# Group normalization that streams 268 MB: stores and loads taking turns in runs of three in place of two

## The chip, the cores and the metric

The kernel runs on one core of a Trainium2 chip, beside no other work. The metric is the device time of one execution in microseconds (us).

The instruction queues that matter are TensorE (PE, matmul), VectorE (DVE), ScalarE (ACT), GpSimd (POOL) and SyncE (SP). SP issues all large transfers. The transfers themselves are carried out by 16 DMA engines, each of which works through its own part of every transfer in the order of issue. A transfer has landed when the last of the 16 has finished its part.

## The reference, cut to what matters

```python
B, C, H, W = 128, 1024, 32, 16          # bfloat16
xr  = x.reshape(B, 32, 32, H, W)        # 32 groups of 32 channels
mu  = xr.mean(axis=(2, 3, 4), keepdims=True)
var = ((xr - mu) ** 2).mean(axis=(2, 3, 4), keepdims=True)
xn  = (xr - mu) / jnp.sqrt(var + 1e-5)
return xn.reshape(B, C, H, W) * g[None, :, None, None] + b[None, :, None, None]
```

The input is 134.2 MB and so is the output. One row of 16,384 values (one sample, one group) lies on one partition, so a tile of 128 partitions is four samples, 4.19 MB, and there are 32 tiles.

## The kernel before

Each tile is loaded, its mean is taken on PE and DVE, its squares about the mean on ACT, and it is scaled in place by DVE, POOL and ACT and stored. There are six tile buffers, so load `i + 6` has to wait until store `i` has landed. "Quarters" means that a tile is moved by four transfers of a quarter each; the squares of the first and of the last tile, which are loaded in quarters, are taken about the first quarter's mean, so that ACT can start early (`shifted`).

```python
XBUFS = 6
UPFRONT = 6
RUN = 2
...
def L(i):                                  # load tile i, issued by SP
    xt = xpool.tile([P, F], BF16, name="xt")
    parts = NQ if i == 0 or i >= NT - 1 else 1
    w = F // parts
    for c in range(parts):
        chain("sp", nc.sync.dma_start(out=xt[:, c*w:(c+1)*w], in_=x_v[i][:, c*w:(c+1)*w]))
    state[i] = {"xt": xt}

for i in range(min(UPFRONT, NT)):          # six loads before anything else
    L(i)
...
def shifted(i):
    return i == 0 or i == NT - 1
...
def M(i):                                  # 32 matmuls with an identity: sums on PE
    if shifted(i):
        matmuls(st, "pa", 0, MQ); matmuls(st, "pb", MQ, NMM)
    else:
        matmuls(st, "pa", 0, NMM)
...
def finish(i):
    if i < 0 or in_parts(i):               # the last two tiles are stored in quarters by A
        return
    for k in range(KC - LAST_SHARE, KC):
        scale_on("act", i, k)
    S(i, 0, NQ)                            # store tile i, issued by SP
    state.pop(i)
    if i % RUN == RUN - 1:
        first = i + 1 + UPFRONT - RUN
        for j in range(first, min(first + RUN, NT)):
            L(j)

M(0); R0(0); GB(); R1(0)
for i in range(NT):
    Q(i)                                   # squares on ACT; calls finish(i - 1) in its middle
    if i + 1 < NT:
        M(i + 1)
        R0(i + 1)                          # mean of the NEXT tile, on DVE
    V(i)                                   # 1/sqrt, scale and shift of tile i
    A(i)                                   # scaling of tile i
```

`chain` keeps the written order on each queue. SP's order is therefore: loads 0 to 5, stores 0 and 1, loads 6 and 7, stores 2 and 3, loads 8 and 9, and so on to loads 30 and 31, and then the last six stores.

Of the kernel before, what the change touches and what calls it, by code (L numbers as in the profile page):

```python
# [16 lines left out]

XBUFS = 6
UPFRONT = 6
RUN = 2  # L20
MM_FREE = 512
QUARTERS = 4
STORE_IN_PARTS = 2
# [6 lines left out]
def kernel(  # L30
# [21 lines left out]
    NT = B0 // NS  # L52
# [5 lines left out]
    NQ = QUARTERS  # L58
# [26 lines left out]
    def chain(key, inst):  # L85
        prev = last.get(key)
        if prev is not None:
            tc.add_manual_dep(inst.ins, prev.ins.name, nosync, reason="pipeline order")
        last[key] = inst
        return inst  # L90

    state = {}

    def L(i):
        xt = xpool.tile([P, F], BF16, name="xt")
        parts = NQ if i == 0 or i >= NT - 1 else 1
        w = F // parts
        for c in range(parts):
            chain(
                "sp",  # L100
                nc.sync.dma_start(  # L101
                    out=xt[:, c * w : (c + 1) * w], in_=x_v[i][:, c * w : (c + 1) * w]
                ),
            )
        state[i] = {"xt": xt}

    for i in range(min(UPFRONT, NT)):
        L(i)
# [35 lines left out]
    def GB():  # L144
# [9 lines left out]
            ),  # L154
        )
        chain("dve", nc.vector.tensor_copy(out=gb[:], in_=gb_p[:]))  # L156

    def shifted(i):
        return i == 0 or i == NT - 1

    def matmuls(st, name, lo, hi):
        ps = pspool.tile([P, MMN], F32, name=name)
# [13 lines left out]
    def M(i):  # L176
        st = state[i]
        if shifted(i):
            matmuls(st, "pa", 0, MQ)
            matmuls(st, "pb", MQ, NMM)  # L180
        else:
            matmuls(st, "pa", 0, NMM)
# [18 lines left out]
    def R0(i):  # L201
        st = state[i]
        if shifted(i):
            st["q"] = sum_of(st["pa"], None, "q")
        else:
            st["negmean"] = sum_of(st["pa"], None, "negmean")

    def R1(i):
        st = state[i]
        if not shifted(i):  # L210
            return
        st["negmean"] = sum_of(st["pb"], st["q"][:], "negmean")
        off = spool.tile([P, 1], F32, name="off")
        chain(
            "pool",
            nc.gpsimd.tensor_scalar(  # L216
                out=off[:],
                in0=st["negmean"][:],
                scalar1=1.0 / NQ,
                scalar2=st["q"][:],  # L220
                op0=ALU.mult,
                op1=ALU.subtract,
            ),
        )
        seed = spool.tile([P, 1], F32, name="seed")
        chain(
            "pool",
            nc.gpsimd.tensor_scalar(
                out=seed[:],
                in0=off[:],  # L230
                scalar1=-1.0,
                scalar2=off[:],
                op0=ALU.mult,
                op1=ALU.mult,
            ),
        )
        st["seed"] = seed
# [17 lines left out]
    def Q(i):  # L255

        st = state[i]
        if shifted(i):
            sq = spool.tile([P, NQ], F32, name="sq")
            for k in range(NQ):  # L260
                squares(st, QF, k, st["q"][:], 1.0 / NQ, sq[:, k : k + 1])
                if k == 0:
                    finish(i - 1)
            st["sq"] = sq
            return
        s0 = spool.tile([P, 1], F32, name="s0")
        s1 = spool.tile([P, 1], F32, name="s1")
        squares(st, F // 2, 0, st["negmean"][:], 1.0, s0[:])
        v0 = spool.tile([P, 1], F32, name="v0")
        finish(i - 1)  # L270
        chain(
            "pool",
            nc.gpsimd.tensor_scalar(  # L273
                out=v0[:],
                in0=s0[:],
                scalar1=inv_n,
                scalar2=EPS,
                op0=ALU.mult,
                op1=ALU.add,
            ),  # L280
        )
        squares(st, F // 2, 1, st["negmean"][:], 1.0, s1[:])
        st["v0"], st["s1"] = v0, s1
# [73 lines left out]
    def scale_on(key, i, k):  # L357
        st = state[i]
        span = st["xt"][:, k * HW : (k + 1) * HW]
        scl = st["scl"][:, k : k + 1]  # L360
        bia = st["bia"][:, k : k + 1]
        if key == "act":
            inst = nc.scalar.activation(  # L363
                out=span, in_=span, func=ACT.Identity, bias=bia, scale=scl
            )
        else:
            eng = nc.vector if key == "dve" else nc.gpsimd
            inst = eng.tensor_scalar(  # L368
                out=span,
                in0=span,  # L370
                scalar1=scl,
                scalar2=bia,
                op0=ALU.mult,
                op1=ALU.add,
            )
        chain(key, inst)

    def S(i, lo, hi):
        chain(
            "sp",  # L380
            nc.sync.dma_start(
                out=o_v[i][:, lo * QF : hi * QF],
                in_=state[i]["xt"][:, lo * QF : hi * QF],
            ),
        )

    def in_parts(i):
        return i >= NT - STORE_IN_PARTS
# [19 lines left out]
    def finish(i):  # L408
        if i < 0 or in_parts(i):
            return  # L410
        for k in range(KC - LAST_SHARE, KC):
            scale_on("act", i, k)
        S(i, 0, NQ)
        state.pop(i)
        if i % RUN == RUN - 1:
            first = i + 1 + UPFRONT - RUN
            for j in range(first, min(first + RUN, NT)):
                L(j)

    M(0)  # L420
# [40 lines left out]
```

## Time and profile before

| | before |
|---|---|
| median time | 633.9 us (633.54 to 634.19, 3 runs) |
| span in the profile | 632.5 us |
| bytes moved | 268.44 MB, half read, half written |
| DMA queue of the kernel's transfers | 99.0% of 16 engines' span |
| ACT busy | 537.9 us, 85% |

These are lines of the page's second and third parts, for the kernel before: the span in 40 equal slices (busy tenths of the DMA engines, then GB/s), then DMA queues with packets, MB and share of 16 engines' span.

```profile
...
DMA  9999999999999999999999999999999999999996
GB/s 371 437 428 406 436 433 431 433 429 433 429 424 433 429 437 431 432 434 433 434 432 424 432 433 431 429 432 432 431 431 431 436 429 432 431 425 435 431 423 260
...
q1 hardware_dynamic: 10944, 268.44, 99.0%
q8 instruction: 8, 0.13, 0.1%
q14 instruction: 15, 0.12, 0.0%
...
```

The DMA engines are busy in every slice, at about 432 GB/s; only the first and the last slice fall off. The queues called "instruction" (q8 and q14) carry the engines' own instructions: few bytes, but they pass through the same 16 engines.

The costliest compute groups of the kernel before follow, with busy us, mean ns of one, then idle time before them and what ended it. ACT spends 427 us in the squares and still stands idle 55 us, waiting for a mean (`jd`), and PE waits 318 us for loads. All compute waits for data.

```profile
...
L244 ACT ACTIVATE ja<-xt,negmean 128x8192 fp8e5<-128x8192 bf16 x60 | 426.6, 7109 | 55.2 <-DVE jd L189 55.1
L166 PE MATMUL pa<-xt,eye 128*128 128x512 bf16 x976 | 250.1, 421 | 317.9 <-DMA xt<-in_x_dram 317.9
...
```

SP's own waits show the other side of the same fact: it waits 453 us for stores to land, because a landed store is what frees a buffer.

```profile
...
SPq L101 <- DMA out_dram<-xt: 453.2, 26, 29.0
SPq L381 <- DVE xt L368: 124.0, 14, 37.0
...
```

I also used the record of every DMA packet. A tile is moved by 128 packets of 32 KB, eight on each engine. The median packet takes 1213 ns, for loads and for stores alike; 16 engines x 32,768 bytes / 1.213 us is 432 GB/s, and 64 tile transfers x 8 packets x 1.213 us is 621 us. The packets of a tile that goes in quarters are of 8 KB and take 309 ns.

### The profile page before, as it was taken

To read this page: it belongs to the slowest core of one execution; us is meant where nothing else is said; L and a number is where in the kernel's file an instruction comes from. 1 tells how busy PE (TensorE), PEld (TensorE's weight loads), DVE (VectorE), ACT (ScalarE), POOL (GpSimd) and SP (SyncE) were. 2 spreads that over 40 slices of the span, in tenths; PEclk is the share of its full clock that TensorE was granted. 3 is DMA by queue.
4 is the path that set the end of the run, shared out by engine and by line. 5 is a ranking of instruction groups with operands and counts; after the bars stand their busy time and mean duration, and the time that the engine had idled before them with its cause. 6 is when DMAs were issued, how large, how long until landed. Compare 5 with 4: busy or idle time off the path is not lost.

```text
span 632.5 us, 3907 instructions
## 1 busy us (share of the span) xinstructions
PE 260.9 (41%) x1025; PEld 106.4 (17%) x1025; DVE 379.0 (60%) x645; ACT 537.9 (85%) x268; POOL 345.3 (55%) x523
## 2 busy tenths in 40 slices
PE   5577609064180632806327063270723607146000
PEld 2223203021030210302113021030301203012000
DVE  1077766666676477563665636666466663657660
ACT  4599999999999699696996969969798796987960
POOL 0077776666666377563665636666365663657100
PEclk9789759668595675957759577595875958758555
DMA  9999999999999999999999999999999999999996
GB/s 371 437 428 406 436 433 431 433 429 433 429 424 433 429 437 431 432 434 433 434 432 424 432 433 431 429 432 432 431 431 431 436 429 432 431 425 435 431 423 260
DMA packets 11063, 268.70 MB, mean 425 GB/s; under 512 B 1312, under 2 KB 1312, under 8 KB 1312
## 3 DMA queue, kind: packets, MB, share of 16 engines
q1 hardware_dynamic: 10944, 268.44, 99.0%
q8 instruction: 8, 0.13, 0.1%
q14 instruction: 15, 0.12, 0.0%
q10 hardware_dynamic: 96, 0.00, 0.0%
HBM read 134.22 MB, written 134.22 MB: 424 GB/s over the span
## 4 chain that ended last, share of the span: by engine, by line
DMA 62%; ACT 15%; PE 9%; issue 5%; DVE 3%; POOL 2%; SPq 0%; DVEq 0%; ACTq 0%; POOLq 0%
DMA out_dram<-xt 40%; DMA xt<-in_x_dram 21%; ACT ja L244 13%; PE pa L166 9%; DVE xt L368 3%; ACT xt L363 2%; POOL xt L368 1%; DMA gb_b<-in_g_dram 0%; ACT rstd L308 0%; POOL scl L337 0%; POOL shift L343 0%; POOL bia L353 0%; SPq L101 0%; DVE rstd L312 0%; DVE jd L189 0%
## 5 line engine op out<-in xcount | busy, mean ns | idle before, releaser
L244 ACT ACTIVATE ja<-xt,negmean 128x8192 fp8e5<-128x8192 bf16 x60 | 426.6, 7109 | 55.2 <-DVE jd L189 55.1
L166 PE MATMUL pa<-xt,eye 128*128 128x512 bf16 x976 | 250.1, 421 | 317.9 <-DMA xt<-in_x_dram 317.9
L368 DVE TENSOR_SCALAR xt<-xt,scl,bia 128x512 bf16<-128x512 bf16 x536 | 351.4, 730 | 39.8 <-POOL bia L353 39.8
L368 POOL TENSOR_SCALAR xt<-xt,scl,bia 128x512 bf16<-128x512 bf16 x390 | 307.5, 801 | 3.4 <-POOL bia L353 0.3
L166 PEld LDWEIGHTS <-eye 128*128 128x128 bf16 x1024 | 106.3, 106 | 472.2 <-DMA xt<-in_x_dram 318.8
L337 POOL TENSOR_SCALAR scl<-gb,rstd 128x32 f32<-128x32 f32 x31 | 11.1, 358 | 220.1 <-DVE rstd L312 220.1
L189 DVE TENSOR_SCALAR_CACHE_REDUCE jd<-pa 128x512 bf16<-128x512 f32 x32 | 21.9, 684 | 113.9 <-PE pa L166 113.9
L363 ACT ACTIVATE xt<-xt,bia,scl 128x512 bf16<-128x512 bf16 x98 | 72.0, 799 | 0.8 <-DVE bia L324 0.8
L312 DVE RECIPROCAL rstd<-rstd 128x1 f32<-128x1 f32 x32 | 5.2, 163 | 72.7 <-ACT rstd L308 72.7
L244 ACT ACTIVATE ja<-xt,q 128x4096 fp8e5<-128x4096 bf16 x8 | 29.7, 3706 | 6.6 <-DVE jd L189 6.4
L343 POOL TENSOR_SCALAR shift<-scl,negmean 128x32 f32<-128x32 f32 x31 | 11.1, 358 | 3.1
L216 POOL TENSOR_SCALAR off<-negmean,q 128x1 f32<-128x1 f32 x2 | 0.9, 430 | 20.4 <-DVE jd L189 20.4
L166 PE MATMUL pb<-xt,eye 128*128 128x512 bf16 x48 | 11.0, 379 | 0.6 <-DMA xt<-in_x_dram 0.6
L244 ACT ACTIVATION_READ_ACCUMULATOR ja<-xt,negmean 128x1 f32 x60 | 11.2, 187 | 0.0
L308 ACT ACTIVATE rstd<-s,v 128x1 f32<-128x1 f32 x30 | 8.8, 294 | 2.8
L353 POOL TENSOR_TENSOR bia<-shift,gb 128x32 f32<-128x32 f32 x31 | 7.8, 251 | 2.6
L273 POOL TENSOR_SCALAR v<-s 128x1 f32<-128x1 f32 x30 | 5.7, 191 | 2.5
L308 ACT ACTIVATE rstd<-var,eps_t 128x1 f32<-128x1 f32 x2 | 0.6, 294 | 7.5 <-DVE jv L292 7.5
L156 DVE COPY gb<-gb_p 128x64 f32<-128x64 f32 x1 | 0.2, 225 | 5.5 <-PE gb_p L148 5.5
L116 ACT ACT_TABLE_LOAD x1 | 1.3, 1283 | 1.7 <-PEq L445 1.7
L189 DVE DVE_READ_ACCUMULATOR jd<-pa 128x1 f32 x32 | 2.6, 80 | 0.0
L292 DVE TENSOR_SCALAR_CACHE_REDUCE jv<-sq,seed 128x4 f32<-128x4 f32 x2 | 0.4, 214 | 2.7 <-ACT ja L244 2.7
(18 smaller groups left out, 6.1 us busy)
## 6 DMA issues: line engine op xcount, KB each, us to landing
xt<-in_x_dram SPq DMA_DIRECT2D x30, 4096.0 KB, 19.4
out_dram<-xt SPq DMA_DIRECT2D x30, 4096.0 KB, 29.3
xt<-in_x_dram SPq DMA_DIRECT2D x8, 1024.0 KB, 11.5
out_dram<-xt SPq DMA_DIRECT2D x8, 1024.0 KB, 17.9
gb_b<-in_g_dram ACTq DMA_DIRECT2D x1, 2.0 KB, 3.2
gb_b<-in_b_dram ACTq DMA_DIRECT2D x1, 2.0 KB, 5.2
```

What stands on the lines that cost most here:

```text
L116: chain("act", nc.scalar.activation(out=warm[:], in_=eps_t[:], func=ACT.Sqrt))
L166: nc.tensor.matmul(out=ps[:], lhsT=eye[:], rhs=st["xt"][:, k * MMN : (k + 1) * MMN], start=(k == lo), stop=(k == hi - 1),),
L189: nc.vector.tensor_scalar(out=jd[:], in0=ps[:], scalar1=-inv_n, scalar2=seed, op0=ALU.mult, op1=ALU.add, accum_out=total[:],),
L244: nc.scalar.activation(out=ja[:, 0:w], in_=st["xt"][:, k * w : (k + 1) * w], func=ACT.Square, bias=bias, scale=scale, accum_out=sq, satura ...
L273: nc.gpsimd.tensor_scalar(out=v0[:], in0=s0[:], scalar1=inv_n, scalar2=EPS, op0=ALU.mult, op1=ALU.add,),
L308: nc.scalar.activation(out=rstd[:], in_=last_sum[:], func=ACT.Sqrt, bias=bias[:], scale=scale),
L312: chain("dve", nc.vector.reciprocal(out=rstd[:], in_=rstd[:]))
L337: nc.gpsimd.tensor_scalar(out=scl[:], in0=gam, scalar1=rstd[:], scalar2=None, op0=ALU.mult),
L343: nc.gpsimd.tensor_scalar(out=shift[:], in0=scl[:], scalar1=st["negmean"][:], scalar2=None, op0=ALU.mult,),
L353: nc.gpsimd.tensor_tensor(out=bia[:], in0=shift[:], in1=bet, op=ALU.add),
L363: inst = nc.scalar.activation(out=span, in_=span, func=ACT.Identity, bias=bia, scale=scl)
L368: inst = eng.tensor_scalar(out=span, in0=span, scalar1=scl, scalar2=bia, op0=ALU.mult, op1=ALU.add,)
```

## The change

Its intent: turn from storing to loading and back less often. Runs are of three tiles instead of two (the first of two, so that the count comes out). The last group of loads is then 29, 30 and 31, and the quarters with the early squares move from tile 31 to tile 29, the first of that group.

```diff
-RUN = 2
+RUN = 3
+FIRST_RUN = 2
...
+    def shifted(i):
+        return i == 0 or i == NT - RUN
...
-        parts = NQ if i == 0 or i >= NT - 1 else 1
+        parts = NQ if shifted(i) else 1
...
-    def shifted(i):
-        return i == 0 or i == NT - 1
...
-        if i % RUN == RUN - 1:
-            first = i + 1 + UPFRONT - RUN
-            for j in range(first, min(first + RUN, NT)):
+        if i % RUN == FIRST_RUN - 1:
+            done = i + 1 + UPFRONT
+            for j in range(max(UPFRONT, done - RUN), min(done, NT)):
                 L(j)
```

Counting the first group of loads and the last group of stores, the transfers change from loads to stores 14 times before and 10 times after, and from stores to loads 13 and 9 times.

## The prediction

> **What bounds the kernel now.** The DMA engines. Part 2 of the page shows DMA at 9 tenths in 39 of 40 slices and about 432 GB/s; part 3 gives the load/store queue 99.0% of 16 engines' span. The bytes are 268.44 MB, half read, half written. In the packet records nearly every 32 KB packet takes 1213 ns, a load's or a store's alike: 27.0 GB/s per engine, 432 GB/s for 16. A tile is 8 packets per engine, 9.70 us; 64 transfers are 621 us. The Trainium skill ("DMA: Bandwidth & Descriptors", section "Where 436 GB/s comes from") puts the ceiling at 435.2 GB/s, so the trace stands within 1% of it. ACT is busy 85%, but waits 55 us for loaded tiles; per tile it needs about 16.7 us (2 x 7.1 + 2.1 + 0.3), against a DMA period of 19.4.
>
> The 11 us above 621 are: 2 us before the first packet; about 0.7 us because four 8 KB packets of the quartered tiles take 4 x 309 ns instead of 1213; and one late DMA engine. The landings of the 16 engines spread by 0.5 us at 23 us, 2.5 at 100, 7.4 at the end. The spread grows in jumps near the small instruction-fetch packets (8 of 16 KB, about 1.04 us each, and 8 KB ones of 0.31 us). The last slice (260 GB/s) is that engine finishing alone.
>
> **What the change touches.** Read-write turns: 13 store runs followed by loads become 9, so 27 changes of direction become 19. What is one worth? On the late engine, landings are 9.64 to 9.72 us apart with or without a change of direction between them (for instance 103.32, 113.01, 122.64, 132.32), so it costs under 0.05 us: 8 fewer save at most 0.4 us. The queue is never empty now either: a load is issued when an old store lands, with another 9.7 us transfer behind it.
>
> The quarters move from the last tile to tile 29; their number stays. Other instructions stay as they are.
>
> **Can it stall?** A cycle of six transfers is 58 us; ACT needs 50 for its three tiles. At the start, tile 4's store is ready about 112 us (S3 at 95.5 plus 16.7), before the queue would run dry at 122. At the end, counted from the landing of store 25: loads land at 9.7, 19.4, 29.1; stores 26 to 30 fill the queue to 77.6. ACT finishes tile 28 at about 12.5, tile 29 at 30.5, tile 30 at 47.6, tile 31 at 63; its first quarter can be stored at about 67. The quick engines want it at about 70, the late one at 77.6. Tight, but enough.
>
> **Prediction: 633.5 us**, 8 in 10 between 631.6 and 635.4. Faster by over 2% 0.01, within 2% 0.975, slower by over 2% 0.015.
>
> **What would show it.** The span near 632 us; 32 KB packets still 1213 ns; slices still 430 to 435 GB/s; landings on the late engine still about 9.7 us apart; SP's waits for stores about as long in total; median time to landing of stores and loads longer (a transfer stands behind more others) without a longer span; the spread of the landings at the end still about 7 us. If direction changes do cost, the steady slices rise.
>
> **What would make it wrong.** A gap in the queue at the tail (last stores issued after about store 25 + 77 us), or at the first run of three; a fetch pattern that loads another DMA engine, or spreads the fetches, moving the late engine's 7 us; a hidden cost of turning that a quick engine, not the late one, pays.

## More of the kernel before

Last, SP's timeline of the kernel before (start, length of the group, operation). One cycle of two loads and two stores takes about 39 us, and a group of loads takes 10 us to issue, since its second load waits for the next store to land.

```profile
...
230.23 10.01 SPq L101 DMA_DIRECT2D xt<-in_x_dram  x2
240.34 0.85 SPq L381 DMA_DIRECT2D out_dram<-xt  x2
269.62 9.95 SPq L101 DMA_DIRECT2D xt<-in_x_dram  x2
279.67 0.85 SPq L381 DMA_DIRECT2D out_dram<-xt  x2
308.31 9.99 SPq L101 DMA_DIRECT2D xt<-in_x_dram  x2
...
```

## The result, and the profile after

| | before | after |
|---|---|---|
| median time | 634.05 us (4 runs) | 632.84 us (632.57 to 633.15, 4 runs) |
| span in the profile | 632.5 us | 630.9 us |
| ratio | | 0.9985, 95% interval 0.9971 to 0.9999 |
| the same, repeated with 5 rounds | 633.97 us | 632.79 us; 0.9982, 0.9970 to 0.9995 |

A ratio is the mean time of one kernel's fast runs over that of the other's of the same rounds, so not quite the ratio of the medians quoted. The change saves 1.2 us, 0.2%: a small gain that came back in a second set of runs.

The same lines of the kernel after: slices of the span, and the queue of the transfers.

```profile
...
DMA  8999999999999999999999999999999999999996
GB/s 366 432 431 428 433 432 425 434 434 432 427 433 433 430 432 432 431 422 433 431 434 430 431 434 432 430 434 438 424 434 432 439 432 430 423 433 429 434 421 290
...
q1 hardware_dynamic: 10944, 268.44, 99.1%
...
```

The steady slices have not risen, they lie around 431 GB/s as before. The queue's share is 99.1 in place of 99.0%, and the last slice holds 290 GB/s in place of 260: the end is less ragged.

SP's waits of the kernel after:

```profile
...
SPq L382 <- DVE xt L369: 361.8, 29, 37.2
SPq L105 <- DMA out_dram<-xt: 211.2, 26, 11.6
...
```

The wait for landed stores fell from 453 to 211 us. That is no gain: the wait for DVE, which scales the tiles to be stored, rose from 124 to 362 us, and the sum is 573 us in place of 577. SP now has a longer list of stores ahead, so it stands at another place in its list while the same transfers run.

SP's timeline of the kernel after shows the run of three: a cycle of six transfers takes 288.99 - 230.00 = 59.0 us, 9.83 us per transfer; before, 308.31 - 230.23 = 78.1 us for eight transfers is 9.76. Over the whole middle it is 9.74 us after (409.2 us for 42 transfers, from 112.93 to 522.09) and 9.78 before (430.3 us for 44, from 113.08 to 543.36). The pace in the middle is thus the same within 0.4%. That small difference is not nothing: 0.037 us for each of some 44 transfers is 1.6 us, as much as the whole gain. SP issues a load when an old store has landed, so what SP's timeline shows is the pace of the latest DMA engine.

```profile
...
230.00 19.72 SPq L105 DMA_DIRECT2D xt<-in_x_dram  x3
249.89 32.83 SPq L382 DMA_DIRECT2D out_dram<-xt  x3
288.99 19.74 SPq L105 DMA_DIRECT2D xt<-in_x_dram  x3
...
```

Median times from issue to landing (page, sixth part; the last number of each line), first of the kernel before, then of the kernel after, grew as the queue became deeper, without a longer span:

```profile
...
xt<-in_x_dram SPq DMA_DIRECT2D x30, 4096.0 KB, 19.4
out_dram<-xt SPq DMA_DIRECT2D x30, 4096.0 KB, 29.3
...
```

```profile
...
xt<-in_x_dram SPq DMA_DIRECT2D x30, 4096.0 KB, 29.0
out_dram<-xt SPq DMA_DIRECT2D x30, 4096.0 KB, 36.8
...
```

### Where the 1.2 us are: the latest of 16 engines

I put every packet record on one of the 16 engines: on an engine a packet starts within 10 ns of the end of the one before it, and each engine takes the transfers in order, eight packets of each. All 16 get 16.78 MB. The result is safe where few engines run in step; where two engines end packets at the same instant, their names may be swapped. It is my own reckoning, not a view of the profile. It gives this, for the end of the last packet in us:

```
                    quickest engine   middle (8th)   latest engine
before                   623.9            625.6          631.2
after                    623.7            625.3          629.5
after, second set        623.8            625.5          629.8
```

The quickest engine does little but 1213 ns packets: 1.9 us of start, 621.1 us, and 0.7 us for quarters make 623.7. (It too has longer packets at the start and at turns, 1.7 us in all before; they are made up for by packets that start some 3 ns before the one ahead has ended.) It is the same before and after, and so is the middle engine within 0.3 us. The time is set by the latest engines, and these are the ones which moved, the last by 1.4 to 1.8 us. The explanation has to be found there.

It has to hold for more than one engine. In the same records the second latest engine ended only 0.4 us before the latest, at 630.8 us, and had to move too: it ended at 629.1 and 629.6 us in the two sets after. The third moved from 629.1 to 628.0 and 628.1 us.

### The profile page after: what moved, and what is told of

Its sections match the earlier page's. It is cut to its first block, busy times and chain, and to the rows that moved or that the text cites. A ratio compares the mean times of both kernels' runs of the same rounds, so it can differ in the third digit from the quotient of the medians.

```text
span 630.9 us, 3885 instructions
## 1 busy us (share of the span) xinstructions
PE 257.5 (41%) x1005; PEld 106.1 (17%) x1025; DVE 378.9 (60%) x645; ACT 537.6 (85%) x268; POOL 345.2 (55%) x523
## 3 DMA queue, kind: packets, MB, share of 16 engines
q1 hardware_dynamic: 10944, 268.44, 99.1%
## 4 chain that ended last, share of the span: by engine, by line
DMA 66%; DVE 10%; ACT 9%; PE 8%; issue 3%; POOL 1%; SPq 1%; DVEq 0%; POOLq 0%; ACTq 0%
DMA out_dram<-xt 41%; DMA xt<-in_x_dram 25%; DVE xt L369 9%; PE pa L167 8%; ACT ja L245 8%; ACT xt L364 1%; SPq L105 0%; POOL scl L338 0%; POOL shift L344 0%; POOL bia L354 0%; ACT rstd L309 0%; DVE jd L190 0%; DVE rstd L313 0%; SPq L382 0%; DVEq L457 0%
## 5 line engine op out<-in xcount | busy, mean ns | idle before, releaser
L167 PE MATMUL pa<-xt,eye 128*128 128x512 bf16 x957 | 246.4, 418 | 320.1 <-DMA xt<-in_x_dram 317.5
L245 ACT ACTIVATION_READ_ACCUMULATOR ja<-xt,q 128x1 f32 x8 | 1.5, 186 | 0.0
## 6 DMA issues: line engine op xcount, KB each, us to landing
out_dram<-xt SPq DMA_DIRECT2D x30, 4096.0 KB, 36.8
```

Of the source, the lines that this page charges most:

```text
L167: nc.tensor.matmul(out=ps[:], lhsT=eye[:], rhs=st["xt"][:, k * MMN : (k + 1) * MMN], start=(k == lo), stop=(k == hi - 1),),
L245: nc.scalar.activation(out=ja[:, 0:w], in_=st["xt"][:, k * w : (k + 1) * w], func=ACT.Square, bias=bias, scale=scale, accum_out=sq, satura ...
```

## The experiments

All kernels are correct unless it is said that they are wrong. The name before each is that of its record. Groups of runs were made on different chips, so each is set beside the kernel before in its own rounds.

### 1. The two halves of the change, and other run lengths

`e1_run3_last`: the run of three alone, with the quarters left on the last tile.

```diff
 (against the kernel after)
-        return i == 0 or i == NT - RUN
+        return i == 0 or i == NT - 1
```

> Runs of three, but the quarters stay on the last tile: the run length alone. Theory T (a turn from loads to stores costs the engines a little, so fewer turns save about 1 us): as the changed kernel, 632.8 us, ratio 0.998. Theory Q (the saving comes from the quarters' move): as the kernel before, 634.0. The quarters' place should cost nothing in the middle; if the tail is as tight as I reckoned, up to 1 us is lost there, with a gap in the DMA's last slices.

`e2_run2_q29`: the move of the quarters alone.

```diff
 (against the kernel before)
-        parts = NQ if i == 0 or i >= NT - 1 else 1
+        parts = NQ if i == 0 or i == NT - 3 else 1
-        return i == 0 or i == NT - 1
+        return i == 0 or i == NT - 3
```

> Runs of two, the quarters on tile 29: the move of the quarters alone. Theory T: 634.0 us, ratio 1.000 within 0.1%. Theory Q: 632.8.

`e3_run1`: loads and stores one by one.

```diff
 (against the kernel before)
-        if i % RUN == RUN - 1:
-            first = i + 1 + UPFRONT - RUN
-            for j in range(first, min(first + RUN, NT)):
-                L(j)
+        if 1 <= i and i + UPFRONT - 1 < NT:
+            L(i + UPFRONT - 1)
```

> Loads and stores alternate one by one: 26 turns from loads to stores in place of 13 or 9, everything else as before. Theory T: 13 more turns at 0.05 to 0.25 us each for the latest engine: 634.7 to 637 us, with bursts of 32 KB packets longer than 1213 ns at many of them. Rival N (turns cost nothing, the 1.2 us are the chance place of the instruction fetches on the DMA engines): 634 within 0.7.

`e4_run4`: the kernel after with `RUN = 4`.

> Runs of four after a first of two, quarters on tile 28: 7 turns from loads to stores in place of 9. Theory T: another 0.2 to 0.6 us less than the changed kernel, 632.2 to 632.7, if the tail holds; by my reckoning ACT finishes tile 31 some 78 us after store 21 to 25's run ends, where the quick DMA engines want it at 80, so up to 2 us may be lost at the end, seen as a lower last slice. Rival N: 633 to 634 plus that tail loss.

Measured in 5 rounds on one chip, beside 633.74 us for the kernel before:

| run | load-to-store turns | median us | ratio (95%) |
|---|---|---|---|
| e1_run3_last | 10 | 632.29 | 0.9980 (0.9967 to 0.9992) |
| e2_run2_q29 | 14 | 633.75 | 0.9999 (0.9987 to 1.0012) |
| e3_run1 | 27 | 634.11 | 1.0004 (0.9992 to 1.0017) |
| e4_run4 | 8 | 639.56 | 1.0096 (1.0082 to 1.0109) |

The whole gain comes with the run of three; the move of the quarters is worth nothing by itself, and is not needed beside the run of three either. Theory Q is out. Thirteen more turns (e3) cost 0.4 us by the medians, below the range of theory T and inside that of its rival; the interval, up to 1.1 us, just reaches the lower end of theory T. So a turn has no fixed price that explains everything: by the medians hardly anything happens from 27 to 14 turns, and more than 1 us from 14 to 10.

The run of four was expected to win a little or to lose up to 2 us at the end. It lost 5.8 us, and not at the end. These are its slices, SP's timeline and SP's waits:

```profile
...
GB/s 377 436 435 395 433 438 436 432 377 440 436 403 451 405 430 428 423 428 429 432 429 415 432 408 428 448 404 434 396 430 427 424 430 398 439 439 414 433 420 362
...
```

```profile
...
129.53 12.69 SPq L105 DMA_DIRECT2D xt<-in_x_dram  x4
145.82 62.74 SPq L382 DMA_DIRECT2D out_dram<-xt  x4
208.62 12.90 SPq L105 DMA_DIRECT2D xt<-in_x_dram  x4
224.89 62.23 SPq L382 DMA_DIRECT2D out_dram<-xt  x4
287.17 13.51 SPq L105 DMA_DIRECT2D xt<-in_x_dram  x4
...
```

```profile
...
SPq L382 <- DVE xt L369: 501.1, 37, 37.2
SPq L105 <- DMA out_dram<-xt: 79.8, 13, 11.5
...
```

Slices of 377, 395 and 403 GB/s come back through the whole span. A group of four stores now takes 62.7 us to issue (145.82 to 208.6), since SP waits for DVE; the wait for landed stores, which means a full queue, fell to 80 us. The cycle is 287.17 - 208.62 = 78.6 us, where eight transfers need 8 x 9.70 = 77.6. The reason is in the kernel's order. The scaling of a tile comes after the next tile's mean on DVE, so the chain from the landing of load 8 to the issue of store 9 is: matmuls, two tiles on ACT, scaling. That is about 10 + 2 x 16.7 + 12 = 55 us (an estimate from the busy times of the groups), and the trace has 208.6 - 152.3 = 56.3 us. The loads stand behind this store in SP's list, so the queue of the quick DMA engines comes close to empty. It is seldom quite empty: by the packet records each engine stood idle for 1.7 us at most, while the quickest ended 10 us later than before. Most of the loss is in longer packets. The chain of waits of the kernel before shows the first of these terms: the matmuls of a tile take 9.8 us after its load.

```profile
...
464.93 19.32 DMA xt<-in_x_dram
484.25 0.05 issue
484.30 9.76 PE pa L166 x32
...
```

The drained engines also end together, within 1.6 us (634.0 to 635.5), in place of 7.4 us before. And it is then that turns become dear: the load packets just ahead of the later turns are together 62 us longer than 1213 ns each, summed over the engines, against 10 to 15 us before and after. Turns from stores to loads become dear as well: the last packets of the stores ahead of them are together 55 us longer and the first load packets behind them 15 us, where every other kernel here has 1 us or less of each. Why a turn costs this much here is open. This run does not tell what fewer turns alone are worth; it tells where the run length has to stop.

### 2. Turns without arithmetic

Three copies, and later a fourth: the same loads, stores, buffers and order, and no arithmetic at all. Their outputs are wrong, which doesn't matter for the times.

```diff
 (against the kernel after)
-    (everything between the six first loads and the definition of S)
-    (everything from A on)
+    for i in range(NT):
+        if in_parts(i):
+            for c in range(NQ):
+                S(i, c, c + 1)
+            continue
+        S(i, 0, NQ)
+        state.pop(i)
+        (loads after it in runs of 1, 2, 3 or 6, as above)
```

> A copy on purpose, wrong result: the same loads, stores and buffers, no arithmetic at all, loads and stores alternating one by one. It measures turns by themselves, with almost no instruction fetches. If turns cost because all 16 engines turn together, 26 turns at the 1.2 us per engine seen at the first turn give 625 + 30 = 655 us; if only the first turn costs and the later ones 0.1 us, 627 to 630 us; if turns cost nothing, 625 to 626 us, equal for the three copies.

> The same copy in runs of two (13 turns from loads to stores). Turns dear when in step: about 640 us. Only the first dear: 627 to 628. Free: 625 to 626. In all cases the spread of the 16 engines' landings at the end should be under 2 us if the 7 us of the kernel before come from instruction fetches.

> The same copy in runs of three (9 turns). Turns dear when in step: about 635 us. Only the first dear: 627. Free: 625 to 626.

> The copy without arithmetic (wrong on purpose) in runs of six: 6 turns from loads to stores, with the first, against 10, 14 and 27 in runs of three, two and one, which took 630.4, 631.2 and 631.7. T2: four turns fewer at up to 0.25 us on the late engine: 629.4 to 630.2. Rival (runs of three are faster for another reason than the number of turns): 630.4 or more.

| run | load-to-store turns | median us | ratio to the kernel before (95%) | engines' ends, quickest and latest |
|---|---|---|---|---|
| c1_copy | 27 | 631.68 | 0.9966 (0.9951 to 0.9980) | 623.2, 628.6 |
| c2_copy | 14 | 631.15 | 0.9959 (0.9942 to 0.9976) | 623.5, 627.7 |
| c3_copy | 10 | 630.42 | 0.9938 (0.9917 to 0.9958) | 623.4, 627.6 |
| c6_copy | 6 | 629.04 | 0.9919 (0.9906 to 0.9933) | 623.7, 626.2 |

Some lines of the pages of c2_copy and c6_copy: span, slices, queues.

```profile
span 628.9 us, 145 instructions
...
GB/s 369 431 433 415 433 431 433 433 433 433 433 433 433 433 431 433 427 433 423 433 433 431 433 431 433 433 431 433 431 433 434 431 423 440 433 431 433 433 416 307
...
q1 hardware_dynamic: 10944, 268.44, 99.4%
q14 instruction: 1, 0.01, 0.0%
...
```

```profile
span 627.6 us, 123 instructions
...
GB/s 368 434 434 422 432 430 422 434 432 434 434 434 432 434 432 434 434 430 434 426 432 434 434 430 434 432 430 432 430 430 434 434 434 434 432 432 428 432 417 337
...
q1 hardware_dynamic: 10944, 268.44, 99.6%
...
```

This was not what any of my three cases said: all three had put c2_copy and c3_copy either far above or below what came, and the spread of the ends under 2 us. Without one arithmetic instruction the program is only 2.6 us faster than the kernel before (the DMA bound is real), and the latest engine is still 4.2 us behind the quickest with a single instruction fetch in the whole span. So fetches are not the only cause of a late engine. And the times fall with the turns: 2.64 us for 21 turns, 0.13 us each on the average (c6_copy ran on another chip; by the ratios it is 0.14). The intervals of neighbours overlap; those of c1_copy and c6_copy do not. The profiled runs of c2_copy and c3_copy took 630.71 and 630.67 us, so from two to three the copies alone show no clear gain.

The packet records say how a turn costs. For c2_copy, eight of the 14 turns from loads to stores; "spread" is how far the latest engine stands behind the quickest when it begins the store, and the sums are over 16 engines, of what the eight packets of the last load and the eight of the first store took over 1213 ns each:

```
turn          first engine at   spread   last load, over   first store, over
L5  > S0          61.4 us        0.6 us     15.00 us           0.00 us
L7  > S2         100.2           0.6         0.00              0.00
L13 > S8         216.3           1.2         0.91              0.06
L15 > S10        255.1           1.9         2.21              0.04
L17 > S12        293.9           2.8         3.95              0.02
L21 > S16        371.4           3.0         0.63              0.03
L25 > S20        448.8           3.7         1.73              0.03
L31 > S26        565.1           4.2         1.03              0.04
```

The other six turns have 5.3 us between them ahead of the store. Load packets grow, store packets don't, and the packets at turns from stores to loads show nothing either. On one engine the eight packets of load 17 were 0, 0, 0, 0, 0, 0, 960 and 0 ns over. It is the last packet or two of a load, on engines that are still loading while others store already. At the first turn all 16 engines pay about 0.9 us each. Later the bill goes to the few engines that are behind, and it puts them further behind: in c2_copy the four latest paid 2.3 to 3.8 us for the later turns, the other twelve 0.8 us or less. Only the latest engine counts for the time. Why a load packet is slowed there I can't tell from these records, nor why some turns (L7 > S2) cost nothing.

### 3. Instruction fetches

`h_half_pe`: every second matmul of the means left out, wrong (it stays inside the tolerance).

```diff
 (against the kernel after)
-        for k in range(lo, hi):
+        for k in range(lo, hi, 2):
-                    stop=(k == hi - 1),
+                    stop=(k == hi - 2),
 (and the factor of the sum doubled)
```

> The changed kernel with every second matmul of the means left out (wrong on purpose: the means are those of half the channels): 512 matmuls and weight loads fewer. If the 16 KB fetches are TensorE's instructions they fall from 8 to 4. If the late DMA engine is late because of the fetches (1.04 us plus about 0.4 for the next packet each), 2 to 5 us less: 628 to 631 us, and a spread of the last landings of 2 to 4 us in place of 5.8. Rival: the lateness comes from turns or memory, 632.8 us, spread unchanged. ACT gets its means earlier, which should not matter as the DMA bounds.

It took 634.32 us beside 633.74 for the kernel before: ratio 1.0004 (0.9989 to 1.0019). The rival was nearer, and even it had expected 632.8 us. Its page:

```profile
...
GB/s 373 435 431 419 429 433 429 431 431 433 427 436 431 433 434 433 435 433 432 433 430 429 429 431 428 429 431 437 432 433 435 433 423 420 438 431 434 433 414 246
...
q14 instruction: 15, 0.12, 0.0%
q8 instruction: 4, 0.07, 0.0%
...
```

The q8 fetches fell from 8 to 4, so the 16 KB fetches are TensorE's. But the time did not fall. On the engines, the reason is plain: each 16 KB fetch falls on another DMA engine, once, and none of these was the engine that ends last. The latest one (631.3 us) had six fetches of 8 KB, 117 us apart, and 3.6 us of lengthened load packets at turns, where it had 1.7 us in the kernel after (second set). Why the turns were dearer in this kernel is open.

These are 13 of the 15 fetches of 8 KB by engine in the kernel before, with the start in us and by how many ns the next packet on the engine was longer than 1213 (left out where only the 4-byte end mark of a transfer came next):

```
end of engine   its fetches of 8 KB
631.2           71 +354   172 +575   281 +536   398 +552   516 +621   611
627.1           72        188        320 +221   439 +234   579 +202
626.8           103 +173
625.6           533 +192
```

The latest engine takes six fetches of one stream. Each holds it for 309 ns and lengthens the packet behind it by another 350 to 620 ns, 4.9 us in all (with 383 ns behind the end mark at 611 us). The two fetches that the table leaves out came at 303 us (+227) and at 363 us (+419), the latter on the second latest engine, its only one. In the kernel after (second set) the same row reads 70 +354, 172 +358, 291 +351, 408 +455, 524 +463, 608 +396, 4.2 us in all. In that row all six fell into a run of stores and cost the next packet 351 to 463 ns; in the kernel before, four fell into a run of loads and cost it 536 to 621. The other profiles repeat this: in e2_run2_q29 four met loads and cost 548 to 660 ns, in e1_run3_last all six met stores and cost 351 to 463. The run length thus also changed what those fetches met, and this is worth some 0.6 to 0.9 us on their engine.

`d_half_dve`: whose fetches are they? VectorE scales two channels by one instruction, wrong (the second with the first one's factors).

```diff
 (against the kernel after)
-            for k in range(KC - LAST_SHARE - POOL_SHARE):
-                scale_on("dve", i, k)
+            for k in range(0, KC - LAST_SHARE - POOL_SHARE, 2):
+                scale_on("dve", i, k, 2)
```

> The changed kernel, wrong on purpose: VectorE scales two channels by one instruction (the second with the first's factors), so it has 8 in place of 16 scaling instructions a tile. Theory F (the six 8 KB fetches about 118 us apart that all fall on one DMA engine are VectorE's instructions, and cost that engine 0.31 us and about 0.45 us of the next packet each): three of the six go, the engine that had them ends about 2.3 us earlier, and the time falls by 0.3 to 1.5 us, as far as the next late engine allows. Rival (the fetches belong to another engine or do no harm): 632.8, six such fetches as before.

It took 632.63 us, ratio 0.9978 (0.9965 to 0.9992), beside 632.79 us for the kernel after in the same rounds. The page has two fetches fewer on q14 than the 15 of the kernels before and after:

```profile
...
q8 instruction: 8, 0.13, 0.1%
q14 instruction: 13, 0.11, 0.0%
...
```

By engine, the six became four (87, 274, 466 and 596 us), some 190 us apart instead of 118, so they are VectorE's; I had expected three, but a tile still has the other instructions. Their engine now ended at 628.1 us, 1.7 us earlier. The time fell by only 0.16 us, because another engine, which has one fetch, ended at 629.5. Theory F is right about the cause, and the gain is below its range.

That other engine, the second latest of the kernel before, shows a third burden, which no run explains: in the kernels with arithmetic one engine's store packets take 20 to 60 ns more in many of the stores (about 4.6 us in all before), and no engine's do in the copies. By the same records this sum was about 0.9 us smaller in the kernel after (second set) than before, and with it goes most of what this engine gained; turns and fetches moved it by 0.2 us only.

### 4. Quarters that have no use

`b_whole_tail`:

```diff
 (against the kernel after)
-STORE_IN_PARTS = 2
+STORE_IN_PARTS = 1
-        return i == 0 or i == NT - RUN
+        return i == 0
```

> The changed kernel without the quarters that have no use by the runs so far: tile 29 loads whole with the plain mean, tile 30 is stored whole; tile 0 and the last store stay in quarters. Four 8 KB packets take 4 x 309 ns in place of 1213, so each whole tile saves 8 x 23 ns on every engine, 0.37 us for the two: 632.3 to 632.5 if the tail has the room that the run of three with the quarters on the last tile showed. If the tail is tight: 633 or more, with a lower last slice.

It took 632.64 us, ratio 0.9980 (0.9968 to 0.9993); the kernel after, in the same rounds (`r_after`), 632.79 us:

> The changed kernel once more, unedited, so that the next two stand beside it on one chip, and for a second look at its packets. 632.8 us, ratio 0.998 to 0.9985. New theory T2, from the packet records so far: a turn from loads to stores lengthens the last load packets of those engines that are still loading while others store already, about 0.25 us a turn on a late engine, and 9 turns in place of 13 save about 1 us of that. If T2 is right, the lengthened packets at turns are load packets again and store packets stay at 1213 ns.

The packet records of `r_after` agree with theory T2 in kind, for it is load packets that grow: over the nine later turns the last loads took 10.7 us more than 1213 ns each, summed over the engines, the first stores 2.1, nearly all of that on one engine with slow stores throughout. They don't show that fewer turns cost less in all: by the same records this sum is 14.4 and 12.3 us in the profiles with runs of two (before, e2), 11.6 and 13.2 in those of the kernel after and e1, and 15 to 18 in the other three with runs of three (h, d, b).

For the kernel with whole tiles, the expected 0.37 us came out as 0.15, which these rounds can't tell from nothing. The slices show why it is no clear win:

```profile
...
GB/s 368 433 429 426 431 433 428 433 433 433 429 431 433 430 433 433 436 422 431 431 433 432 431 433 433 432 433 433 431 433 433 431 430 433 433 423 430 431 364 366
...
```

The next to last slice is 364 in place of 421 GB/s. Store 30 is now ready late, and the quick engines stand idle for up to 4.7 us at the end; the late ones do not notice. It is not clearly better than the kernel after, nor is e1_run3_last (632.29 us on another chip). Nothing that I ran beats both kernels by more than the noise.

## Why the prediction was right or wrong

The time, 632.84 us, lies inside 631.6 to 635.4, and "within 2%" was right. That follows from the DMA bound. It says little about turns: the range is 3.8 us wide and the change was worth 1.2, so a free turn and one several times dearer than foretold both fit into it. Point by point:

1. **The DMA engines bound the kernel.** Right. The copy without arithmetic takes 631.2 us, 0.4% less than the kernel before.
2. **"it costs under 0.05 us: 8 fewer save at most 0.4 us."** Wrong, and this is the term that was mis-sized. I had read a few landings in a row (103 to 132 us) in which nothing happened. The copies put a turn from loads to stores at 0.13 us on the average, with single ones from 0 to 1 us on a late engine. A turn from stores to loads was free, as predicted, in runs of up to three and in the copies, though not in the run of four. In the kernel the run of three saved 1.2 to 1.5 us in three sets of runs, where I had allowed 0.4.
3. **One late engine, late because of instruction fetches.** Half right. In the kernel before, 4.9 of the 7.4 us by which it trails are six fetches of VectorE and the packets behind them; 2.2 us are load packets at later turns. Without fetches the latest engine of c2_copy still trails by 4.2 us. And the 16 KB fetches, which I had put first, did not set the time: in the kernel before none falls on the two latest engines, and half of them taken away gained nothing.
4. **"the spread of the landings at the end still about 7 us"** Wrong: 7.4 became 5.8 and 6.0 us, and this difference is about the gain.
5. **The tail is tight, but enough.** Right. I had ACT finish tile 31 at 63 us after the landing of store 25, which was at 541.6 us, so at 604.6. In ACT's timeline of the kernel after, its squares end at 602.7:

```profile
...
595.48 7.12 ACT L245 ACTIVATE ja<-xt,negmean 128x8192 fp8e5<-128x8192 bf16 x1
602.50 0.19 ACT L245 ACTIVATION_READ_ACCUMULATOR ja<-xt,negmean 128x1 f32 x1
602.78 0.29 ACT L309 ACTIVATE rstd<-s,v 128x1 f32<-128x1 f32 x1
603.92 5.75 ACT L364 ACTIVATE xt<-xt,bia,scl 128x512 bf16<-128x512 bf16 x8 [0.84 <-DVE bia L325]
```

   In SP's timeline the twelve last stores are all issued within 70.0 us of 542.09, that is by 612.1 us, before the late engine needs them.

```profile
...
522.09 19.89 SPq L105 DMA_DIRECT2D xt<-in_x_dram  x6
542.09 70.03 SPq L382 DMA_DIRECT2D out_dram<-xt  x12
```

6. **SP's waits for stores "about as long in total".** Wrong as written: 453 became 211 us. The sum with the wait for DVE stayed, as shown above; the name of a wait moved, not the work.
7. **Times to landing longer, slices and packets unchanged.** Right: loads 19.4 to 29.0 us, stores 29.3 to 36.8 us, slices around 431 GB/s, packets of 1213 ns.

What is shown: the run length alone carries the gain, it lies on the latest engine, and fewer load-to-store turns, from 27 to 6, shorten a program that does nothing else. What is only argued is how the 1.2 us divide inside the kernel. The copies give 0.7 us from runs of two to runs of three (with overlapping intervals). On the latest engine (before, and after in its second set) the later turns differ by 0.6 us, the first turn by 0.35 and the fetches with the packets behind them by 0.6; on the second latest it is mostly the slow stores. Single profiles are too noisy to settle it: the first turn comes before the two programs differ, and still differs by that much. That four turns fewer are the cause of the gain in the kernel is thus not shown; the run length changes the turns, the place of the fetches and the slow stores together. A run that shifts VectorE's fetches by one tile with a few idle instructions, without touching the turns, would tell.

## What to carry to other kernels

When all DMA engines are busy, look for the latest of the 16 and not at the mean: a few small things that always fall on one engine (instruction fetches, the last load packets at a turn) set the end. Longer runs of loads and of stores help a little, as long as the queue never runs dry; one step too far, here four tiles, lost four times what three had won. Before giving a cost as zero because a few intervals look even, measure it over the whole span or in a copy that does nothing else.

## What the Trainium skill lacked or had wrong

- "DMA: Bandwidth & Descriptors", section "Where 436 GB/s comes from", gives 435.2 GB/s as the ceiling and says that for transfers between HBM and SBUF the HBM side (about 358) binds, though it mentions a measurement of 425 beside that. With one core alone, this case moved 425 GB/s before and 426 after over the whole span and 432 GB/s at the rate of a 1213 ns packet, loads and stores alike. "HBM Reference", section "Specifications (TRN2)", has the right number for a core alone (about 425).
- No page tells the cost of turning between directions. Here a turn from loads to stores lengthened the last load packets in flight, by up to 1 us on single engines and about 0.9 us on all 16 at the first turn, 0.13 us per turn in the time of a copy; from stores to loads nothing was seen, except in the run of four, where the last store packets were 55 us longer in sum.
- "Runtime: NRT & Kernel Launch", section "Instruction fetch mechanics", says that instructions are refilled in blocks of 16 KiB and that the cost is mostly hidden. Only TensorE's were of 16 KB here; VectorE's were of 8 KB. The page speaks of the engine that waits for its instructions; the DMA engine that carried them did pay: 309 ns and 350 to 620 ns more for the packet behind each, all six on one engine, 4.9 us in the kernel before.
- "DMA: Bandwidth & Descriptors", section "Queues, rings and completion order", lists instruction refills under row 14. Here TensorE's 16 KB fetches came on q8, as the profile numbers the queues, four or eight of them as the matmuls were halved or not, and each on another DMA engine.
- No page tells of a DMA engine whose store packets alone are 20 to 60 ns longer while the core computes (about 4.6 us in all before); the cause is open.
